# Attention and gated feed-forward on one core: an accumulator on the normalise, sums by column, probability remainders on GpSimd, weight words merged in PSUM, and twelve leading weight blocks

## The chip, the cores and the metric

The kernel runs on one NeuronCore of a Trainium2 chip. The metric is the device time of one execution in microseconds; the median of several runs counts. The engines are named as in the profile: PE is TensorE (PEld its weight loads), DVE is VectorE, ACT is ScalarE, POOL is GpSimd, and SP is SyncE, which issues the DMAs.

## The reference

Eight batches with eight heads of width 64. Each batch has 512 local tokens, which attend to the 32 global tokens and to local tokens within 32 positions, and 32 global tokens, which attend to everything. The result, 544 tokens by 512 per batch, goes through a gated feed-forward layer of width 1536.

```
sm(s):  e = exp(s - max(s));  e / (sum(e) + 1e-9)
out_g = sm(scale * q_g k_all^T) v_all
out_l = sm([scale * q_l k_g^T, scale * q_l k_l^T where |i - j| <= 32 else -1e9]) [v_g; v_l]
x     = all heads of a token side by side
out   = (sigmoid(x w_gate) * (x w_val)) w_out
```

The three weights are fp64 values of which the kernel receives the bits; all else is fp32.

## The kernel before, in words

**Precision.** A product in full fp32 is slow on TensorE, so most operands are split: a "hi" part, rounded to the type float32r by ScalarE, and a "lo" part, the remainder, by a subtraction on GpSimd (`hh lo`, `xt lo`, `k lo`, `q lo`, `v lo`, `p lo`, `w lo`). Three products (hi hi, lo hi, hi lo) replace one.

**Work.** The tokens form chunks: chunk 0 is the first 256 tokens of batch 0, chunk 1 the other 256 with the batch's global tokens, chunks 2 to 8 are batches 1 to 7 of 512 tokens, and at the end come the 256 global tokens of all batches. For each chunk attention makes `xt` (the hi and lo parts of x, transposed), and the feed-forward stream runs over 12 weight blocks f of 128 columns: gate products into `bank_g`, value products into `bank_v` (L705), then the output products of the block before into `bank_o` (L719). While TensorE streams the feed-forward of one chunk, the attention of the next one is woven in.

**Attention of a head** has local units of two blocks of 128 queries (`local_unit`), and a `global_unit`. In the first heads (chunks 0 and 1, half of chunk 2: 24 units, "native") all is in fp32, and TensorE transposes the probabilities. The other 104 units run: scores on PE (L338); mask, scaling and maximum on DVE, which writes `s_buf` and, through its accumulator, `nm` (L376); exponential on ACT with the row sums in `sm` (L389); then the step `norm` on DVE: add 1e-9 to both sums (L433), reciprocal (L434), multiply each block by its reciprocal (L436 twice, 192 or 224 columns), transpose in 32 by 32 blocks into `tb` (L438). Four DMAs write `tb` to DRAM and two read it back as `pt` (L444, L449). ACT takes the hi part (L452), the step `p lo` subtracts it (L454; on DVE for the first unit of a head, on POOL for the second), and PE multiplies by the values (L462, L463). Then ACT copies, DVE adds (L468) and POOL adds (L470) into x.

**Weights.** `convert(i)` turns 36 blocks of fp64 words into fp32 at the start: a DMA brings 512 KB into a part of the tile `xt`; DVE masks the sign (L230) and merges the low word (L231), ACT rescales the high word (L233), DVE merges it (L235); ACT takes the hi part (L242) and POOL the lo part (L244). The output weight's parts go to DRAM (`wo_dram`) and are loaded again for each use (L668).

**The order.** `Order` is a planner that runs when the program is built: each piece of work yields steps with an engine, an assumed duration in us and the buffers it takes and gives, and the planner always begins the step that can start first, with ties by rank. The assumed durations decide how the instructions of each engine are interleaved; on the chip each engine then runs its list in that order. Lines that matter here:

```
LEAD = 8                     # blocks f of chunk 0, then of chunk 1, before the two alternate
items = [(chs[0], f) for f in range(LEAD)] + [(chs[1], f) for f in range(LEAD)]
for f in range(LEAD, NF):    # NF = 12
    items += [(chs[0], f), (chs[1], f)]
RANK = {"split": 1.0, "conv": 15.0, "products": 5.0}
```

Of the kernel before, what the change touches and what calls it, by code (L numbers as in the profile page):

```python
# [16 lines left out]
P = 128  # L17
# [5 lines left out]
KWIN = (192, 224, 224, 192)  # L23
# [122 lines left out]
def kernel(ctx, tc, qk, v, w_gate, w_val, w_out, out_l, out_g):  # L146
    nc = tc.nc
# [12 lines left out]
    ps = ctx.enter_context(tc.tile_pool(name="ps", bufs=1, space=PSUM))  # L160
# [59 lines left out]
    def convert(i):  # L220
        f, kind = divmod(i, 3)
        yield step("load w", "SP", 0.4, take=[f"words{i % 3}"], lat=4.6)
        src = conv_bufs[i % 3]
        nc.sync.dma_start(src, w_src[i])
        yield step("word", "DVE", 0.35 + 0.62, take=[f"out{i % 2}"])
        pairs = src.rearrange("p (n two) -> p n two", two=2)
        low, high = pairs[:, :, 0], pairs[:, :, 1]
        w = conv_out[i % 2]
        wf, hf = w.bitcast(F32), high.bitcast(F32)
        nc.vector.tensor_scalar(w, high, 0x80000000, None, op0=ALU.bitwise_and)  # L230
        nc.vector.scalar_tensor_tensor(w, low, 29, w, op0=ALU.logical_shift_right, op1=ALU.bitwise_or)  # L231
        yield step("exponent", "ACT", 0.58)
        nc.scalar.mul(hf, hf, 2.0 ** -112)  # L233
        yield step("word", "DVE", 0.62, give=[f"words{i % 3}"])
        nc.vector.scalar_tensor_tensor(w, high, 3, w, op0=ALU.logical_shift_left, op1=ALU.bitwise_or)  # L235
        yield step("w hi", "ACT", 0.52, take=["ob", "ob"] if kind == 2 else ())
        if kind == 2:
            hi, lo = (ffn.tile([P, 1, DM], F32R, name=nm, tag="ob", bufs=3) for nm in ("wo_hi", "wo_lo"))
        else:
            hi, lo = (t[:, :, f * P:(f + 1) * P] for t in (wg, wv)[kind])  # L240
        wf = wf.rearrange("p (t n) -> p t n", t=hi.shape[1])
        nc.scalar.copy(hi, wf)  # L242
        yield step("w lo", "POOL", 1.35, give=[f"out{i % 2}"])
        nc.gpsimd.tensor_tensor(lo, wf, hi.bitcast(F32), op=ALU.subtract)  # L244
# [95 lines left out]
    def x_part(T, x32s, col0):  # L340
# [3 lines left out]
        prow = 64 * (h % 2)  # L344
        return x32s[h // 2][prow:prow + 64, col0:col0 + 2 * P].rearrange("p (i c) -> p i c", c=P)

    def first_x(T):
        key = "x", T["h"] // 2
        T["group"][key] = T["group"].get(key, 0) + 1
        return ["x32"] if T["group"][key] == 1 else []  # L350

    def local_unit(T, blocks, x32s, col0):
# [17 lines left out]
        else:  # L370
            si = free_s.pop(0)
            s_sb = s_bufs[si]
# [17 lines left out]
                                 accum_out=sm[:, i:i + 1])  # L390
        if nat:
            yield step("sum", "DVE", 0.38)
            nc.vector.tensor_scalar_add(r, sm, 1e-9)
            nc.vector.reciprocal(r, r)
            for i, j in enumerate(blocks):
                yield (st := step("norm", ("DVE", "ACT"), 0.3))
                src = s_sb[:, i, 0:KWIN[j]]
                if st["eng"] == "ACT":
                    nc.scalar.mul(src, src, r[:, i:i + 1])
                else:  # L400
                    nc.vector.tensor_scalar(src, src, r[:, i:i + 1], None, op0=ALU.mult)
            where = f"o{h % 2}" if T["first"] else "att"
            yield step("turn", "PE", 0.46 + (0.43 if T["first"] else 0.0), take=[where])
            pt_ps = bank([P, 4, P], "bank_y", where)
            if T["first"]:
                warm(pt_ps.rearrange("p a c -> p (a c)"), 4)
            for i in range(2):
                nc.tensor.transpose(pt_ps[:, 2 * i], s_sb[:, i, 0:P], ident)
                nc.tensor.transpose(pt_ps[:, 2 * i + 1], s_sb[:, i, WIN - P:WIN], ident)
            own = "th" if T["first"] and h % 2 else "pt"  # L410
            yield step("pt", "ACT", 0.5, take=[own], give=[where, s_res])
            if own == "th":
                pt = ffn.tile([P, 4, P], F32, name="pt_first", tag="th", bufs=2)
            else:
                pt = att.tile([P, 4, P], F32, name="pt_nat", tag="pt", bufs=2)
            nc.scalar.copy(pt, pt_ps)
            if not own_s:
                free_s.append(si)
            where = f"o{2 + h % 2}" if T["first"] else "att"
            yield step("pv", "PE", 1.1, take=[where] + first_x(T), give=[own] + v_over(T), after=[when(("v", ci, h))])  # L420
            vt = T["group"]["v", h]
            o_ps = bank([64, 2, P], "bank_x", where)
            for i, j in enumerate(blocks):
                side = KWIN[j] - (WIN - P)
                nc.tensor.matmul(o_ps[:, i], vt[:, VM[j], :], pt[:, 2 * i], start=True, stop=False)
                nc.tensor.matmul(o_ps[:, i], vt[0:side, VS[j], :], pt[0:side, 2 * i + 1], start=False, stop=True)
            yield step("x", "ACT", 0.3, give=[where])
            nc.scalar.copy(x_part(T, x32s, col0), o_ps)
            mark(("x", ci, h // 2))
            return  # L430

        yield step("norm", "DVE", 0.38 + 0.5 + 0.6, take=["tb"], give=["s"])
        nc.vector.tensor_scalar_add(r, sm, 1e-9)  # L433
        nc.vector.reciprocal(r, r)  # L434
        for i, j in enumerate(blocks):
            nc.vector.tensor_scalar(s_sb[:, i, 0:KWIN[j]], s_sb[:, i, 0:KWIN[j]], r[:, i:i + 1], None, op0=ALU.mult)  # L436
        tb = att.tile([P, 7, 2, 32], F32, name="tb", bufs=2)
        nc.vector.transpose(tb.rearrange("p b k i -> p k b i"), s_sb.rearrange("p k (b i) -> p k b i", i=32))  # L438
        free_s.append(si)
# [7 lines left out]
        for m in range(2):  # L447
# [2 lines left out]
        yield step("p hi", "ACT", 0.52)  # L450
        flat = pt.rearrange("p c m a k i -> p c (m a k i)")
        nc.scalar.copy(flat[:, 0], flat[:, 1].bitcast(F32))  # L452
        yield (st := step("p lo", "POOL" if blocks[0] else "DVE", 0.85 if blocks[0] else 0.8))
        (nc.vector if st["eng"] == "DVE" else nc.gpsimd).tensor_tensor(  # L454
            flat[:, 1], flat[:, 1].bitcast(F32), flat[:, 0].bitcast(F32), op=ALU.subtract)
# [369 lines left out]
```

## Time and profile before

| | before |
|---|---|
| median of 3 runs | 1236.57 us (1235.94 to 1245.51) |
| profiled execution | 1240.92 us, span 1239.2 us |
| PE busy | 1161.9 us, 94% |
| DVE busy | 824.0 us, 66% |
| ACT busy | 785.0 us, 63% |
| POOL busy | 659.9 us, 53% |
| mean granted clock of PE | 0.989 |

The span goes from the first to the last instruction. A busy PE is not PE at its peak, since the ends of matmuls are modelled, so what it waits for is read beside it. In lists of groups a row names line, engine, operation, tiles and count, then busy us, mean ns of one, and the idle time before it with what ended it. The page slices the span; the table of stretches gives the same engine columns for chosen times.

### The profile page before, as it was taken

What the parts mean: (1) busy time and instruction counts of PE and PEld (TensorE: products, weight loads), DVE (VectorE), ACT (ScalarE), POOL (GpSimd) and SP (SyncE); (2) the same over time, 40 slices, a digit from 0 to 9 for tenths busy, and PEclk for the clock granted to TensorE, in tenths of its full rate; (3) what the DMA queues carried; (4) which work ended last, traced back from release to release, by engine and by line L of the source; (5) the groups of instructions that cost most, each with busy time, mean ns of one, the idle gap of its engine ahead of it and who ended that gap; (6) DMA issues with size and microseconds to landing.
All of it is one profiled execution on the core that took longest, in us unless ns stands there. A gap on an engine that the chain in (4) does not pass through costs nothing.

```text
span 1239.2 us, 20480 instructions
## 1 busy us (share of the span) xinstructions
PE 1161.9 (94%) x6236; PEld 946.4 (76%) x6236; DVE 824.0 (66%) x2318; ACT 785.0 (63%) x1844; POOL 659.9 (53%) x683
## 2 busy tenths in 40 slices
PE   9999889898999999999999998999899999999998
PEld 7777668887777777777777776777677777888897
DVE  3578875866875788768776787678776787521121
ACT  4677876766666676767665776667666776522232
POOL 1244444666666576667656666657656676511111
PEclk9998999999999999999999999999999999999999
DMA  6578765656555666566555664566555664321243
GB/s 212 165 242 262 249 204 152 185 164 172 153 168 157 187 179 159 160 179 181 152 149 156 201 183 143 166 173 179 156 153 143 199 192 125 103 87 66 68 137 119
DMA packets 180077, 204.00 MB, mean 165 GB/s; under 512 B 109312, under 2 KB 136960, under 8 KB 179968
## 3 DMA queue, kind: packets, MB, share of 16 engines
q1 hardware_dynamic: 179968, 202.70, 56.0%
q8 instruction: 49, 0.80, 0.3%
q14 instruction: 60, 0.49, 0.1%
HBM read 163.58 MB, written 39.06 MB: 164 GB/s over the span
## 4 chain that ended last, share of the span: by engine, by line
PE 23%; DVE 13%; DMA 12%; issue 9%; ACT 9%; POOL 5%; SPq 4%; DVEq 0%; POOLq 0%; ACTq 0%
PE bank_o L719 8%; PE bank_v L705 6%; PE bank_g L705 6%; DMA pt<-pd 5%; DMA qk_raw<-in_qk_dram 3%; DMA pd<-tb 3%; DVE s_buf L436 2%; ACT qk_hi L280 2%; ACT s_buf L389 2%; SPq L444 2%; DVE r L433 2%; DVE tb L438 2%; SPq L277 1%; POOL kl L283 1%; POOL pt L454 1%
## 5 line engine op out<-in xcount | busy, mean ns | idle before, releaser
L705 PE MATMUL bank_v<-xt,wv 128*128 128x512 f32 (+1 forms) x1440 | 325.9, 366 | 8.6 <-DVE t L468 7.4
L705 PE MATMUL bank_g<-xt,wg 128*128 128x512 f32 (+1 forms) x1440 | 320.6, 365 | 1.7 <-ACT xt L586 1.1
L719 PE MATMUL bank_o<-wo,hh 128*128 128x512 f32 x1224 | 317.2, 398 | 0.3 <-ACT hh L660 0.2
L705 PEld LDWEIGHTS bank_v<-xt,wv 128*128 128x128 f32 x1440 | 241.0, 190 | 55.9 <-DVE t L468 10.5
L705 PEld LDWEIGHTS bank_g<-xt,wg 128*128 128x128 f32 x1440 | 241.8, 190 | 45.9 <-DVE th L657 3.4
L719 PEld LDWEIGHTS bank_o<-wo,hh 128*128 128x128 f32 x1224 | 223.8, 191 | 44.9 <-issue 1.0
L662 POOL TENSOR_TENSOR hh<-th,hh 128x512 fp32r<-128x512 f32 (+1 forms) x120 | 139.3, 1161 | 211.0 <-ACT hh L660 200.4
L656 DVE SCALAR_TENSOR_TENSOR bank_v<-ex,bank_v 128x512 f32<-128x512 f32 (+1 forms) x120 | 72.2, 602 | 140.5 <-PE bank_v L705 135.9
L389 ACT ACTIVATE s_buf<-s_buf,nm 128x192 f32<-128x192 f32 (+1 forms) x248 | 113.9, 461 | 73.3 <-DVE nm L376 72.7
L283 POOL TENSOR_TENSOR kl<-qk_raw,qk_hi 128x736 fp32r<-128x736 f32 x52 | 95.8, 1842 | 111.6 <-ACT qk_hi L280 101.9
L660 ACT CAST hh<-th 128x512 fp32r<-128x512 f32 (+1 forms) x120 | 66.5, 554 | 106.9 <-DVE th L657 105.3
L470 POOL TENSOR_TENSOR x<-t 64x256 f32<-64x256 f32 x104 | 76.0, 730 | 70.1 <-DVE t L468 34.6
L436 DVE TENSOR_SCALAR s_buf<-s_buf,r 128x192 f32<-128x192 f32 x208 | 106.0, 550 | 3.6
L645 ACT ACTIVATE th<-bank_g 128x512 f32<-128x512 f32 (+1 forms) x120 | 63.8, 532 | 68.1 <-PE bank_g L705 66.1
L376 DVE CUSTOM_DVE_ANT_0 s_buf<-bank_x,masks 128x192 f32<-128x192 f32 (+1 forms) x248 | 81.3, 363 | 26.9 <-PE bank_x L338 25.6
L462 PE MATMUL bank_x<-pt,vhl 128*128 128x256 f32 x208 | 61.1, 314 | 36.4 <-POOL pt L454 22.1
L468 DVE TENSOR_TENSOR t<-bank_x,t 64x512 f32<-64x512 f32 x104 | 69.6, 669 | 36.6 <-ACT t L466 36.5
L466 ACT COPY t<-bank_x 64x512 f32<-64x512 f32 x104 | 60.6, 583 | 47.2 <-POOL x L470 25.9
L433 DVE TENSOR_SCALAR r<-sm 128x2 f32<-128x2 f32 x104 | 54.5, 524 | 48.5 <-ACT s_buf L389 46.1
L452 ACT CAST pt<-pt 128x512 fp32r<-128x512 f32 x104 | 64.1, 616 | 35.4 <-DMA pt<-pd 34.6
L462 PEld LDWEIGHTS bank_x<-pt,vhl 128*128 128x128 f32 x208 | 39.3, 189 | 59.8 <-POOL pt L454 35.5
L286 POOL TENSOR_TENSOR qk_hi<-qk_raw,qk_hi 64x256 fp32r<-64x256 f32 x104 | 82.0, 808 | 4.1
(122 smaller groups left out, 2057.8 us busy)
## 6 DMA issues: line engine op xcount, KB each, us to landing
wo<-wo_dram SPq DMA_DIRECT2D x116, 512.0 KB, 3.6
qk_raw<-in_qk_dram SPq DMA_DIRECT2D x104, 320.0 KB, 4.7
pt<-pd SPq DMA_DIRECT2D x208, 128.0 KB, 2.6
pd<-tb SPq DMA_DIRECT2D x416, 56.0 KB, 1.8
v_raw<-in_v_dram SPq DMA_DIRECT2D x52, 256.0 KB, 3.3
out_dram<-ob SPq DMA_DIRECT2D x34, 256.0 KB, 4.2
xt<-in_w_gate_dram SPq DMA_DIRECT2D x12, 512.0 KB, 4.1
xt<-in_w_val_dram SPq DMA_DIRECT2D x12, 512.0 KB, 4.6
```

What stands on the lines that cost most here:

```text
L283: nc.gpsimd.tensor_tensor(kl, t[:, K0:Q1], hi[:, K0:Q1].bitcast(F32), op=ALU.subtract)
L286: nc.gpsimd.tensor_tensor(hi[64:128, r], t[64:128, r], hi[64:128, r].bitcast(F32), op=ALU.subtract)
L376: nc.vector.tensor_tensor_reduce(out=s_sb[:, i, 0:w], in0=s_ps[:, i, 0:w], in1=masks[:, m:m + w], scale=-0.125, scalar=3.0e38, op0=ALU.add ...
L389: nc.scalar.activation(s_sb[:, i, 0:w], s_sb[:, i, 0:w], AF.Exp, bias=nm[:, i:i + 1], scale=-1.0, accum_out=sm[:, i:i + 1])
L433: nc.vector.tensor_scalar_add(r, sm, 1e-9)
L436: nc.vector.tensor_scalar(s_sb[:, i, 0:KWIN[j]], s_sb[:, i, 0:KWIN[j]], r[:, i:i + 1], None, op0=ALU.mult)
L462: nc.tensor.matmul(out, vt[:, VM[j], :], pt[:, :, 0, :, i, :], start=True, stop=False)
L470: nc.gpsimd.tensor_tensor(x_part(T, x32s, col0), t0[:, :, 0], t0[:, :, 1], op=ALU.add)
L656: nc.vector.scalar_tensor_tensor(acc, ex, 1.0, acc, op0=ALU.min, op1=ALU.mult)
L662: nc.gpsimd.tensor_tensor(hh[:, 1, 0:ntok], th, hh[:, 0, 0:ntok].bitcast(F32), op=ALU.subtract)
L705: nc.tensor.matmul(acc, w[a][:, t, fs], xt[:, c, t, x0:x0 + ntok], start=n == 0, stop=n == 11)
L719: nc.tensor.matmul(C2["o"][t], ph[:, a, t * P:(t + 1) * P], pwo[:, c], start=f2 == 0 and i == 0, stop=f2 == NF - 1 and i == 2)
```

## The change

1. The sums get 1e-9 by column: two adds of 128x1 instead of one of 128x2 (`invert`), then the reciprocal as before.
2. The normalise on DVE, also that of native units, writes an accumulator too (`normalise`); its sum goes to `sm`, which nobody reads afterwards.
3. `p lo` is on POOL for all 104 units, with an assumed 1.28 us (before 0.85 on POOL, 0.8 on DVE); the step `norm` is assumed to take 1.7 us instead of 1.48.
4. In `convert` the words of blocks f < LEAD are merged in a PSUM bank (`bank_w`, the bank o2 or o3); only the last merge writes the tile in SBUF.
5. LEAD is 12, so chunk 0 runs all its blocks before chunk 1 begins, all 36 blocks of words are merged in PSUM, and no block's output weights serve two chunks from one load. The rank of conversions is 5 instead of 15.

```diff
-LEAD = 8
+LEAD = 12
-RANK = {"split": 1.0, "conv": 15.0, "products": 5.0}
+RANK = {"split": 1.0, "conv": 5.0, "products": 5.0}
...
-        yield step("word", "DVE", 0.35 + 0.62, take=[f"out{i % 2}"])
+        early = f < LEAD
+        part = f"o{2 + i % 2}" if early else f"out{i % 2}"
+        yield step("word", "DVE", 0.45 + 0.69, take=[part])
         w = conv_out[i % 2]
-        nc.vector.tensor_scalar(w, high, 0x80000000, None, op0=ALU.bitwise_and)
-        nc.vector.scalar_tensor_tensor(w, low, 29, w, op0=ALU.logical_shift_right, op1=ALU.bitwise_or)
+        v = ps.tile([P, 512], F32, name="bank_w", tag=f"bank_{part}").bitcast(U32) if early else w
+        nc.vector.tensor_scalar(v, high, 0x80000000, None, op0=ALU.bitwise_and)
+        nc.vector.scalar_tensor_tensor(v, low, 29, v, op0=ALU.logical_shift_right, op1=ALU.bitwise_or)
         yield step("exponent", "ACT", 0.58)
...
-        nc.vector.scalar_tensor_tensor(w, high, 3, w, op0=ALU.logical_shift_left, op1=ALU.bitwise_or)
+        nc.vector.scalar_tensor_tensor(w, high, 3, v, op0=ALU.logical_shift_left, op1=ALU.bitwise_or)
...
+    def invert(r, sums):
+        for i in range(2):
+            nc.vector.tensor_scalar_add(r[:, i:i + 1], sums[:, i:i + 1], 1e-9)
+        nc.vector.reciprocal(r, r)
+
+    def normalise(p, r, total):
+
+        nc.vector.tensor_scalar(p, p, r, None, op0=ALU.mult, op1=ALU.add, accum_out=total)
...
-        yield step("norm", "DVE", 0.38 + 0.5 + 0.6, take=["tb"], give=["s"])
-        nc.vector.tensor_scalar_add(r, sm, 1e-9)
-        nc.vector.reciprocal(r, r)
+        yield step("norm", "DVE", 0.4 + 0.7 + 0.6, take=["tb"], give=["s"])
+        invert(r, sm)
         for i, j in enumerate(blocks):
-            nc.vector.tensor_scalar(s_sb[:, i, 0:KWIN[j]], s_sb[:, i, 0:KWIN[j]], r[:, i:i + 1], None, op0=ALU.mult)
+            normalise(s_sb[:, i, 0:KWIN[j]], r[:, i:i + 1], sm[:, i:i + 1])
...
-        yield (st := step("p lo", "POOL" if blocks[0] else "DVE", 0.85 if blocks[0] else 0.8))
-        (nc.vector if st["eng"] == "DVE" else nc.gpsimd).tensor_tensor(
-            flat[:, 1], flat[:, 1].bitcast(F32), flat[:, 0].bitcast(F32), op=ALU.subtract)
+        yield step("p lo", "POOL", 1.28)
+        nc.gpsimd.tensor_tensor(flat[:, 1], flat[:, 1].bitcast(F32), flat[:, 0].bitcast(F32), op=ALU.subtract)
```

How the instructions stand now is shown at three places; in each fence the line numbers are those of its own kernel. First DVE, the `norm` step of a unit in the middle of the program, before:

```order
L433 TENSOR_SCALAR r<-sm 128x2
L434 RECIPROCAL r<-r 128x2
L436 TENSOR_SCALAR s_buf_106<-s_buf_106,r 128x224
L436 TENSOR_SCALAR s_buf_106<-s_buf_106,r 128x192
L438 STREAM_TRANSPOSE tb<-s_buf_106 128x2x7x32
```

And with the change, at the same unit:

```order
L353 TENSOR_SCALAR r<-sm 128x1 x2
L354 RECIPROCAL r<-r 128x2
L358 TENSOR_SCALAR s_buf_106,sm<-s_buf_106,r 128x224
L358 TENSOR_SCALAR s_buf_106,sm<-s_buf_106,r 128x192
L449 STREAM_TRANSPOSE tb<-s_buf_106 128x2x7x32
```

The sums are two instructions, and each normalise has a second output.

Second POOL, in the middle of the program, from one `p lo` (pt) to the next, before:

```order
L454 TENSOR_TENSOR pt<-pt 128x512
L662 TENSOR_TENSOR hh<-th,hh 128x512
L470 TENSOR_TENSOR x_4489<-t_4533 64x256
L502 TENSOR_TENSOR xg_113<-y 64x32
L283 TENSOR_TENSOR kl<-qk_raw,qk_hi 128x736
L571 TENSOR_TENSOR ptg<-ptg_buf,ptg 128x5x32
L470 TENSOR_TENSOR x_4489<-t_4617 64x256
L286 TENSOR_TENSOR qk_hi<-qk_raw,qk_hi 64x256
L286 TENSOR_TENSOR qk_hi<-qk_raw,qk_hi 64x288
L454 TENSOR_TENSOR pt<-pt 128x512
```

And with the change:

```order
L465 TENSOR_TENSOR pt<-pt 128x512
L581 TENSOR_TENSOR ptg<-ptg_buf,ptg 128x5x32
L290 TENSOR_TENSOR qk_hi<-qk_raw,qk_hi 64x256
L290 TENSOR_TENSOR qk_hi<-qk_raw,qk_hi 64x288
L465 TENSOR_TENSOR pt<-pt 128x512
L480 TENSOR_TENSOR x_5488<-t_5642 64x256
L672 TENSOR_TENSOR hh<-th,hh 128x512
L318 TENSOR_TENSOR vhl<-v_raw,vhl 128x8x64
L480 TENSOR_TENSOR x_5488<-t_5705 64x256
L512 TENSOR_TENSOR xg_113<-y 64x32
L465 TENSOR_TENSOR pt<-pt 128x512
```

POOL's list now has a `p lo` for each unit, two in a head, between the same other subtractions and adds.

Third PE, the probability products of one unit (pt by vhl) among the feed-forward of the third 512-token chunk, before:

```order
L719 MATMUL bank_o_6581<-wo,hh 128x512
L705 MATMUL bank_g<-xt,wg_114 128x512 x4
L462 MATMUL bank_x<-pt,vhl 128x256
L463 MATMUL bank_x<-pt,vhl 128x256
L462 MATMUL bank_x<-pt,vhl 128x256
L463 MATMUL bank_x<-pt,vhl 128x256
L705 MATMUL bank_g<-xt,wg_115 128x512 x4
L479 MATMUL bank_x<-ptg,vhl 128x64
```

And with the change, at the same rows of the list:

```order
L729 MATMUL bank_o_6684<-wo,hh 128x512
L715 MATMUL bank_g<-xt,wg_114 128x512 x4
L715 MATMUL bank_g<-xt,wg_115 128x512 x4
L472 MATMUL bank_x<-pt,vhl 128x256
L473 MATMUL bank_x<-pt,vhl 128x256
L472 MATMUL bank_x<-pt,vhl 128x256
L473 MATMUL bank_x<-pt,vhl 128x256
L489 MATMUL bank_x<-ptg,vhl 128x64
```

The four products stand behind one more group of four gate matmuls; the unit before this one moved by one group of four value matmuls in the same way. Scores stand where they stood.

More of the change, by code (lines that the diff above doesn't have):

```diff
@@ L224, in convert @@
         nc.sync.dma_start(src, w_src[i])
-        yield step("word", "DVE", 0.35 + 0.62, take=[f"out{i % 2}"])
         pairs = src.rearrange("p (n two) -> p n two", two=2)
         low, high = pairs[:, :, 0], pairs[:, :, 1]
+        hf = high.bitcast(F32)
+        early = f < LEAD
+        part = f"o{2 + i % 2}" if early else f"out{i % 2}"
+        yield step("word", "DVE", 0.45 + 0.69, take=[part])
         w = conv_out[i % 2]
-        wf, hf = w.bitcast(F32), high.bitcast(F32)
-        nc.vector.tensor_scalar(w, high, 0x80000000, None, op0=ALU.bitwise_and)
-        nc.vector.scalar_tensor_tensor(w, low, 29, w, op0=ALU.logical_shift_right, op1=ALU.bitwise_or)
+        v = ps.tile([P, 512], F32, name="bank_w", tag=f"bank_{part}").bitcast(U32) if early else w
+        nc.vector.tensor_scalar(v, high, 0x80000000, None, op0=ALU.bitwise_and)
+        nc.vector.scalar_tensor_tensor(v, low, 29, v, op0=ALU.logical_shift_right, op1=ALU.bitwise_or)
         yield step("exponent", "ACT", 0.58)
         nc.scalar.mul(hf, hf, 2.0 ** -112)
-        yield step("word", "DVE", 0.62, give=[f"words{i % 3}"])
-        nc.vector.scalar_tensor_tensor(w, high, 3, w, op0=ALU.logical_shift_left, op1=ALU.bitwise_or)
+        yield step("word", "DVE", 0.69, take=[f"out{i % 2}"] if early else [], give=[f"words{i % 3}"] + ([part] if early else []))
+        nc.vector.scalar_tensor_tensor(w, high, 3, v, op0=ALU.logical_shift_left, op1=ALU.bitwise_or)
+        wf = w.bitcast(F32)
         yield step("w hi", "ACT", 0.52, take=["ob", "ob"] if kind == 2 else ())
@@ L400, in local_unit @@
                 else:
-                    nc.vector.tensor_scalar(src, src, r[:, i:i + 1], None, op0=ALU.mult)
+                    normalise(src, r[:, i:i + 1], sm[:, i:i + 1])
             where = f"o{h % 2}" if T["first"] else "att"
@@ L430, in local_unit @@
             return
-        yield step("norm", "DVE", 0.38 + 0.5 + 0.6, take=["tb"], give=["s"])
-        nc.vector.tensor_scalar_add(r, sm, 1e-9)
-        nc.vector.reciprocal(r, r)
+        yield step("norm", "DVE", 0.4 + 0.7 + 0.6, take=["tb"], give=["s"])
+        invert(r, sm)
         for i, j in enumerate(blocks):
-            nc.vector.tensor_scalar(s_sb[:, i, 0:KWIN[j]], s_sb[:, i, 0:KWIN[j]], r[:, i:i + 1], None, op0=ALU.mult)
+            normalise(s_sb[:, i, 0:KWIN[j]], r[:, i:i + 1], sm[:, i:i + 1])
         tb = att.tile([P, 7, 2, 32], F32, name="tb", bufs=2)
```

## The prediction

> **What bounds the kernel now.** I read the engine totals first, then three stretches of the span (the weight conversion, the long middle, the tail without attention), and then what TensorE waited for in the middle.
>
> ```profile
> span 1239.2 us, 20480 instructions
> PE 1161.9 (94%) x6236; PEld 946.4 (76%) x6236; DVE 824.0 (66%) x2318; ACT 785.0 (63%) x1844; POOL 659.9 (53%) x683
> ```
>
> ```profile
> 0.00:200.00 200.00, 184.97 (x1097) 146.85 (x1098) 133.48 (x370) 142.32 (x383) 75.63 (x83) 0.96 0.68 214
> 200.00:1062.00 862.00, 804.42 (x4251) 653.81 (x4251) 651.81 (x1877) 586.13 (x1339) 547.42 (x562) 0.99 0.60 167
> 1062.00:1240.00 178.00, 172.51 (x890) 145.70 (x889) 38.70 (x73) 56.56 (x124) 36.87 (x39) 1.00 0.28 95
> ```
>
> The columns are PE, PEld, DVE, ACT and POOL busy, granted clock, DMA share and GB/s. TensorE sets the time, and the change leaves its matmuls alone, so a gain can come only from its idle time and lowered clock. In the middle that is 862.0 - 804.4 = 57.6 us of idle time plus 0.01 x 862, about 9 us, of clock; in the first 200 us it is 15.0 us plus 0.04 x 200 = 8 us. The tail has 5.5 us, and nothing there is touched.
>
> ```profile
> PE bank_x L462 <- POOL pt L454: 22.1, 32, 2.9
> PE bank_x L462 <- issue: 10.8, 13, 1.3
> PE bank_v L705 <- DVE t L468: 7.4, 7, 1.5
> PE bank_x L462 <- DVE pt L454: 3.1, 4, 1.5
> ```
>
> These are the largest waits of TensorE between 200 and 1062 us (us, times, longest). L462 is the first matmul of probabilities by values. Its three rows make 36.0 us, most of the 57.6. It ends a long chain: scores, reduce, exponential, normalise and transpose (VectorE), two trips through DRAM, high part (ScalarE), remainder (L454). TensorE's order is fixed beforehand, so whenever this chain is later than its step times foresaw, all matmuls behind L462 stand still.
>
> Why is it late? The next rows give durations as minimum/median/maximum ns.
>
> ```profile
> L433 DVE TENSOR_SCALAR r<-sm x104: 160/507/1726, 201.6 to 1058.5; 128x2 f32<-128x2 f32 x104
> L436 DVE TENSOR_SCALAR s_buf<-s_buf,r x208: 305/337/1373, 202.0 to 1059.6; 128x192 f32<-128x192 f32 x52, 128x224 f32<-128x224 f32 x52
> L454 DVE TENSOR_TENSOR pt<-pt x52: 684/693/2219, 212.0 to 1066.8; 128x512 fp32r<-128x512 f32 x52
> L438 DVE STREAM_TRANSPOSE tb<-s_buf x104: 645/645/648, 203.2 to 1060.0; 128x448 f32<-128x448 f32 x104
> L547 DVE TENSOR_SCALAR mg<-sg x64: 131/142/145, 60.4 to 1064.1; 32x1 f32<-32x1 f32 x64
> L468 DVE TENSOR_TENSOR t<-bank_x,t x104: 643/674/684, 217.4 to 1072.9; 64x512 f32<-64x512 f32 x104
> L454 POOL TENSOR_TENSOR pt<-pt x52: 1255/1288/1312, 217.6 to 1068.4; 128x512 fp32r<-128x512 f32 x52
> ```
>
> The first three spread by a factor of three to ten on equal work; the next three do not spread at all. What the first three have in common is that all their large operands lie in SBUF. One place shows what they wait for:
>
> ```profile
> 750.71 0.48 DVE L433 TENSOR_SCALAR r<-sm 128x2 f32<-128x2 f32 x1
> 751.43 2.51 DVE L436 TENSOR_SCALAR s_buf<-s_buf,r 128x192 f32<-128x192 f32 x2
> 753.98 0.65 DVE L438 STREAM_TRANSPOSE tb<-s_buf 128x448 f32<-128x448 f32 x1
> 751.25 1.29 POOL L454 TENSOR_TENSOR pt<-pt 128x512 fp32r<-128x512 f32 x1
> 752.50 1.31 POOL L662 TENSOR_TENSOR hh<-th,hh 128x512 fp32r<-128x512 f32 x1
> ```
>
> Two normalises, at least 0.31 + 0.32 us, take 2.51 us and end just after the two GpSimd subtractions beside them (751.25 to 753.81). VectorE is held for whole GpSimd instructions. The means give the price:
>
> ```profile
> L433 DVE TENSOR_SCALAR r<-sm 128x2 f32<-128x2 f32 x104 | 54.5, 524 | 48.5 <-ACT s_buf L389 46.1
> L436 DVE TENSOR_SCALAR s_buf<-s_buf,r 128x192 f32<-128x192 f32 x104 | 56.4, 542 | 1.8
> L436 DVE TENSOR_SCALAR s_buf<-s_buf,r 128x224 f32<-128x224 f32 x104 | 58.0, 557 | 1.8
> L434 DVE RECIPROCAL r<-r 128x2 f32<-128x2 f32 x104 | 17.2, 166 | 3.6
> L454 DVE TENSOR_TENSOR pt<-pt 128x512 fp32r<-128x512 f32 x52 | 45.1, 867 | 10.7 <-ACT pt L452 10.3
> ```
>
> A unit's step from L433 to L438 is 0.52 + 0.17 + 0.54 + 0.56 + 0.65 = 2.44 us; without holding it is 0.16 + 0.17 + 0.31 + 0.33 + 0.65 = 1.62. So 0.82 us per unit, 85 us over 104 units, is holding, and the step time that set the order was 1.48.
>
> **The change part by part.** *Normalise and sums.* Two column adds replace one pair add: by L547 about 0.14 each, so 0.30 with the second's start. The accumulating normalise is not in the trace. To bound it I compare two SBUF instructions of the conversion:
>
> ```profile
> L230 DVE TENSOR_SCALAR xt<-xt x36: 407/424/1868, 12.7 to 171.8; 128x512 uint32<-128x512 uint32 x36
> L231 DVE SCALAR_TENSOR_TENSOR xt<-xt x36: 691/693/1672, 13.1 to 173.7; 128x512 uint32<-128x512 uint32 x36
> ```
>
> L231 handles the same 512 columns 0.27 us slower, 0.53 ns a column. If the accumulating form also falls to that rate, the normalises become 0.31 + 0.10 = 0.41 and 0.33 + 0.12 = 0.45, plus the read of the accumulator:
>
> ```profile
> L376 DVE DVE_READ_ACCUMULATOR2_ANT nm<- 128x1 f32 x256 | 20.9, 82 | 0.0
> ```
>
> At 0.08 each, of which one is hidden, the unit is 0.30 + 0.17 + 0.41 + 0.45 + 0.08 + 0.65 = 2.06 us if nothing holds it, against 2.44: **0.38 us less**, 40 us in all. The ends are 0.82 less (full rate, no holding) and 0.44 more (slow rate and all the holding as now). I take 0.38, because the accumulating reductions on L376 show no holding in their rows (0.33 to 0.39 us), though they read PSUM.
>
> [...]
>
> *Remainders.* 52 subtractions leave VectorE (0.867 us each, 45 us) for GpSimd at 1.288, so these units' chains get 0.42 us longer, and GpSimd's middle goes from 547 to about 614 of 862 us, 71%. The step times now say 1.28 where the GpSimd half was planned at 0.85. In the order, at the place shown with the change, both probability matmuls stand one group of four feed-forward matmuls later, 4 x 0.233 = 0.93 us (the tail runs twelve in 2.80 us):
>
> ```profile
> 1083.30 2.80 PE bank_v L705 x12
> ```
>
> *What TensorE gets back in the middle.* A head has two units. Its chains give back 2 x 0.38 and lose 0.42, which leaves 0.34 us; where the matmuls also stand up to 0.93 us later, up to 1.9 us per head is covered. Today the L462 waits are 36.0 / 52 = 0.69 us per head. I take three quarters of them, 27 us. Of the other 21.6 us of idle time I take 8, since VectorE's middle loses about 80 of 652 us and it frees the score and value banks (L705 behind L468). Of the 9 us of clock I take 4, on the guess that its dips follow long waits. Together **-39 us**; the bounds are nothing and the whole 66.
>
> *The conversion.* Its three word instructions and the sums on native heads are held too:
>
> ```profile
> L230 DVE TENSOR_SCALAR xt<-xt 128x512 uint32<-128x512 uint32 x36 | 22.7, 631 | 24.7 <-DMA xt<-in_w_gate_dram 12.7 <-POOL wg L244 10.2 <-POOL wo_lo L244 1.5
> L231 DVE SCALAR_TENSOR_TENSOR xt<-xt 128x512 uint32<-128x512 uint32 x36 | 29.6, 823 | 1.2
> L235 DVE SCALAR_TENSOR_TENSOR xt<-xt 128x512 uint32<-128x512 uint32 x36 | 29.5, 826 | 10.8 <-ACT xt L233 10.8
> 80.00:180.00 100.00, 90.11 (x588) 68.12 (x587) 87.14 (x215) 82.62 (x223) 45.39 (x40) 0.95 0.78 243
> ```
>
> Means of 0.631, 0.823 and 0.826 against about 0.42, 0.69 and 0.68 make 0.49 us per word block, 18 us over 36. Writing PSUM is not shown for them; if the first falls to L231's rate it costs 0.27 x 36 = 10 us. So VectorE, 87% busy here, gains 8 to 18 us. With LEAD at 12 chunk 0 needs all 36 blocks before chunk 1 starts, and four more loads of 512 KB are issued:
>
> ```profile
> wo<-wo_dram SPq DMA_DIRECT2D x116, 512.0 KB, 3.6
> ```
>
> At the 243 GB/s of this stretch they are 4 x 2.2 = 9 us of transfers, hidden by the 22% of free DMA time unless they queue ahead of weight loads. I take **-8 us** of the 23 on offer, bounds +8 to -18.
>
> Sum: -47 us. The profiled execution took 1240.92 us, its span and 1.7 around it, so 1194; it lies 4.35 above the median of the runs, so the forecast is **1190 us**.
>
> **The rivals.** *GpSimd becomes the bound (slower).* Place: the remainder of the units that ran on VectorE. It is 71% busy then and works in order, and there the subtraction stands behind hh, kl and qk_hi work (the order shows it; the pt and hh rows above give 1.3 us). If each of the 52 waits one such instruction more, say 1.3 us, its chain gets 1.7 us longer while the head's two normalises give back 0.76 and the later place 0.93. From there on more waiting goes straight to TensorE: at 2.2 us of extra waiting it is 0.9 x 52 = 47 us lost against perhaps 20 gained elsewhere, so 1264 us. For it: L462 waits for POOL seven times as long as for DVE. Against it: GpSimd in the middle still waits over a third of the time, and its step time is now right. Chance 7%.
>
> *The accumulating form is held as well.* Then only the sums (0.22 x 104 = 23 us of VectorE), the removed subtraction and the better step time count, while slower normalises take 23 us back: about -8 us, 1229 us. Chance 8%. *DMA keeps the chain late.* The chain's DRAM trips stay:
>
> ```profile
> pt<-pd SPq DMA_DIRECT2D x208, 128.0 KB, 2.6
> pd<-tb SPq DMA_DIRECT2D x416, 56.0 KB, 1.8
> ```
>
> If those are what L462 really ends on, half the middle's gain goes, 1210 us: 20%. *Waits nearly vanish*, since planned and real times now agree everywhere: -85 us, about 1152: 7%.
>
> **How the numbers follow.** My forecast has 58%, DMA 20%, vanishing waits 7%, held accumulation 8%, GpSimd 7%. The range is 1155 to 1225: it takes in the forecast with its bounds and the DMA case and leaves the two unfavourable cases and the far end of the favourable one outside, some 2 in 10. A measurement here tells 1%, 12 us, from no change (1224 to 1249). Faster 0.85 (the first three cases), same 0.08, slower 0.07.
>
> **What would show it.** In the profile after: the accumulating normalise at 0.4 to 0.46 us with hardly any spread, column adds at 0.14; VectorE busy near 720 us (824 less 40, 45 and about 18) and GpSimd near 715 (660 plus 67, less its own share of the holding); L462 waiting under 15 us in all; the granted clock nearer 1 in the first 200 us. I am wrong if normalises still reach 1.3 us, if the waits on L454 grow while GpSimd never idles, or if L705 waits for weight blocks of f = 8 to 11 before chunk 1.

## The result, and the profile after

The changed kernel takes **1195.36 us** (median of 4 runs, 1192.61 to 1199.26) against 1236.40 before: a ratio of 0.9653, 95% interval 0.9599 to 0.9708. The forecast was 1190, its range 1155 to 1225. Run again later, beside the experiments, the same kernel took 1196.83 us (1187.77 to 1202.50), ratio 0.9667 [0.9609, 0.9724]. Medians are over all runs; a ratio and its interval are estimated from the runs that do not count as slow, and are not the quotient of the medians. The profiled execution took 1192.61 us.

The engine totals of the page after:

```profile
span 1190.8 us, 20839 instructions
PE 1142.7 (96%) x6236; PEld 943.1 (79%) x6236; DVE 722.7 (61%) x2625; ACT 778.6 (65%) x1842; POOL 708.2 (59%) x735
```

VectorE fell from 824.0 to 722.7 us and GpSimd rose from 659.9 to 708.2 (forecast 720 and 715). The same three stages after, in the columns of the table before (PE, PEld, DVE, ACT and POOL busy, clock, DMA share, GB/s):

```profile
0.00:190.00 190.00, 181.00 (x1125) 144.56 (x1126) 125.92 (x431) 143.88 (x389) 74.08 (x85) 0.98 0.69 228
190.00:1013.00 823.00, 788.44 (x4222) 652.23 (x4221) 558.70 (x2125) 577.95 (x1329) 596.00 (x610) 0.99 0.64 177
1013.00:1191.00 178.00, 173.23 (x893) 146.31 (x892) 38.04 (x73) 56.73 (x125) 38.10 (x40) 0.99 0.28 95
```

The middle lasts 823 us instead of 862, minus 39, and the stage ahead of it ends some 10 us sooner; the tail is as long as before. TensorE idles 34.6 us in the middle, where it idled 57.6. Only 23 of the 39 us are therefore idle time; the other 16 stood in the column of busy PE (804.4 before, 788.4 now), whose matmul ends are modelled. The two windows do not hold quite the same matmuls (4251 and 4222). Counted from the first feed-forward matmul of chunk 2 (266.4 and 257.0 us) to the same ends, with 3788 and 3785 matmuls, the stretch lost 39.6 us: 25.2 idle and 14.4 busy.

What TensorE waits for after, over the whole span (us, times, longest):

```profile
PE bank_x L472 <- POOL pt L465: 21.7, 20, 3.1
PE bank_g L715 <- DVE th L667: 3.3, 3, 1.1
PE bank_o L729 <- DVE ob L687: 2.5, 3, 1.0
...
PE bank_v L715 <- DVE t L478: 1.9, 4, 0.6
```

L472 is what L462 was. Its three rows made 36.0 us; one is left, with 21.7. The wait for GpSimd alone has hardly changed (22.1 before).

The instructions that the change writes anew (count, minimum/median/maximum ns, first and last start, shapes):

```profile
L353 DVE TENSOR_SCALAR r<-sm x256: 131/154/157, 16.3 to 1009.3; 128x1 f32<-128x1 f32 x128
L358 DVE TENSOR_SCALAR_CACHE_REDUCE s_buf<-s_buf,r x225: 396/425/449, 17.2 to 1010.1; 128x224 f32<-128x224 f32 x57, 128x192 f32<-128x192 f32 x56
L358 DVE DVE_READ_ACCUMULATOR s_buf<-s_buf,r x225: 71/83/90, 17.6 to 1010.4; 128x1 f32 x113
L465 POOL TENSOR_TENSOR pt<-pt x104: 1256/1292/1311, 199.8 to 1020.5; 128x512 fp32r<-128x512 f32 x104
L233 DVE TENSOR_SCALAR bank_w<-xt x36: 662/689/696, 12.4 to 152.2; 128x512 uint32<-128x512 uint32 x36
L234 DVE SCALAR_TENSOR_TENSOR bank_w<-xt,bank_w x36: 695/695/701, 13.2 to 152.9; 128x512 uint32<-128x512 uint32 x36
L238 DVE SCALAR_TENSOR_TENSOR xt<-xt,bank_w x36: 656/680/689, 23.0 to 154.4; 128x512 uint32<-128x512 uint32 x36
```

Each minimum is close to its maximum. Before, the pair add ran up to 1.73 us, the normalise to 1.37 and the word instructions to 1.87. One place shows the normalise beside GpSimd:

```profile
746.08 1.29 POOL L465 TENSOR_TENSOR pt<-pt 128x512 fp32r<-128x512 f32 x1
746.14 0.41 DVE L358 TENSOR_SCALAR_CACHE_REDUCE s_buf<-s_buf,r 128x192 f32<-128x192 f32 x1
...
746.48 0.44 DVE L358 TENSOR_SCALAR_CACHE_REDUCE s_buf<-s_buf,r 128x224 f32<-128x224 f32 x1
...
746.97 0.65 DVE L449 STREAM_TRANSPOSE tb<-s_buf 128x448 f32<-128x448 f32 x1
```

Both normalises run inside one GpSimd subtraction that reads and writes SBUF, and neither side is longer for it. Over the whole trace 115 of the 229 normalises lie inside GpSimd arithmetic with at least 95% of their length and take 0.426 us on average; 42 lie outside it with at least 95% and take 0.422.

### The profile page after: what moved, and what is told of

It is laid out like the page before. It is cut to its first block, busy times and chain, and to the rows that moved or that the text cites. A ratio compares the mean times of both kernels' runs of the same rounds, so it can differ in the third digit from the quotient of the medians.

```text
span 1190.8 us, 20839 instructions
## 1 busy us (share of the span) xinstructions
PE 1142.7 (96%) x6236; PEld 943.1 (79%) x6236; DVE 722.7 (61%) x2625; ACT 778.6 (65%) x1842; POOL 708.2 (59%) x735
## 5 line engine op out<-in xcount | busy, mean ns | idle before, releaser
L715 PE MATMUL bank_v<-xt,wv 128*128 128x512 f32 (+1 forms) x1440 | 321.9, 365 | 3.8 <-DVE t L478 1.9
L729 PE MATMUL bank_o<-wo,hh 128*128 128x512 f32 x1224 | 321.3, 398 | 4.0 <-DVE ob L687 2.5
L715 PEld LDWEIGHTS bank_v<-xt,wv 128*128 128x128 f32 x1440 | 238.6, 190 | 49.2 <-DVE mg L550 5.0
L672 POOL TENSOR_TENSOR hh<-th,hh 128x512 fp32r<-128x512 f32 (+1 forms) x120 | 135.0, 1125 | 186.6 <-ACT hh L670 171.0
L465 POOL TENSOR_TENSOR pt<-pt 128x512 fp32r<-128x512 f32 x104 | 134.2, 1291 | 55.0 <-ACT pt L463 47.8
L287 POOL TENSOR_TENSOR kl<-qk_raw,qk_hi 128x736 fp32r<-128x736 f32 x52 | 92.5, 1778 | 33.7 <-ACT qk_hi L284 29.1
L480 POOL TENSOR_TENSOR x<-t 64x256 f32<-64x256 f32 x104 | 76.1, 732 | 48.2 <-DVE t L478 17.8
L318 POOL TENSOR_TENSOR vhl<-v_raw,vhl 128x512 fp32r<-128x512 f32 x52 | 67.1, 1290 | 44.6 <-ACT vhl L316 36.5
L358 DVE TENSOR_SCALAR_CACHE_REDUCE s_buf<-s_buf,r 128x192 f32<-128x192 f32 (+1 forms) x225 | 88.2, 427 | 3.9
L463 ACT CAST pt<-pt 128x512 fp32r<-128x512 f32 x104 | 64.0, 616 | 39.3 <-DMA pt<-pd 39.2
L667 DVE SCALAR_TENSOR_TENSOR th<-th,bank_v 128x512 f32<-128x512 f32 (+1 forms) x120 | 73.0, 608 | 15.5 <-ACT th L658 5.8
L290 POOL TENSOR_TENSOR qk_hi<-qk_raw,qk_hi 64x256 fp32r<-64x256 f32 x104 | 78.4, 775 | 4.1
```

What stands on the lines that cost most here:

```text
L287: nc.gpsimd.tensor_tensor(kl, t[:, K0:Q1], hi[:, K0:Q1].bitcast(F32), op=ALU.subtract)
L290: nc.gpsimd.tensor_tensor(hi[64:128, r], t[64:128, r], hi[64:128, r].bitcast(F32), op=ALU.subtract)
L358: nc.vector.tensor_scalar(p, p, r, None, op0=ALU.mult, op1=ALU.add, accum_out=total)
L465: nc.gpsimd.tensor_tensor(flat[:, 1], flat[:, 1].bitcast(F32), flat[:, 0].bitcast(F32), op=ALU.subtract)
L480: nc.gpsimd.tensor_tensor(x_part(T, x32s, col0), t0[:, :, 0], t0[:, :, 1], op=ALU.add)
L667: nc.vector.scalar_tensor_tensor(th, th, 1.0, acc, op0=ALU.add, op1=ALU.mult)
```

## The experiments

Each was run in three rounds beside the kernel before, whose median was 1235.31 us with the first four, 1236.49 with the next three and 1235.13 with the last four. Line numbers are those of the changed kernel, except where the kernel before was edited.

### One part undone: the accumulator, the column sums

```diff
-        nc.vector.tensor_scalar(p, p, r, None, op0=ALU.mult, op1=ALU.add, accum_out=total)
+        nc.vector.tensor_scalar(p, p, r, None, op0=ALU.mult)
```

> The changed kernel with its normalise without the accumulator; every engine's order is that of the changed kernel, so only the form of 229 instructions differs. Theory (holding by GpSimd): normalises are held again, mean 0.55 to 0.65 us with maxima over 1.2, against 0.41 and 0.44; VectorE about 20 us busier; 1195 becomes about 1212 us (1205 to 1225). Rival (the new order brought the gain): within 5 us of 1195, since uncontended normalises are shorter without the accumulator (0.32 against 0.43).

Measured: 1214.18 us (1209.25 to 1216.37), ratio 0.9826 [0.9766, 0.9885]. The normalise, in the same order of instructions:

```profile
L358 DVE TENSOR_SCALAR s_buf<-s_buf,r x225: 306/339/2017, 17.4 to 1034.2; 128x224 f32<-128x224 f32 x57, 128x192 f32<-128x192 f32 x56
```

The result is what my theory expected, except that VectorE is 29 us busier (751.3 against 722.7) where 20 were expected. The minimum is 0.09 us shorter than with the accumulator, the maximum 1.6 us longer.

```diff
-        for i in range(2):
-            nc.vector.tensor_scalar_add(r[:, i:i + 1], sums[:, i:i + 1], 1e-9)
+        nc.vector.tensor_scalar_add(r, sums, 1e-9)
```

> The changed kernel with one 128x2 add for both sums instead of two 128x1 adds; same order on every engine. Theory (holding): the add means 0.5 us with maxima over 1.2, against 2 x 0.15; about 0.2 us more on each of 128 units' chains; 1195 becomes 1203 us (1198 to 1212). Rival (the order hides it): within 4 us of 1195.

Measured: 1215.46 us (1212.66 to 1216.71), ratio 0.9839 [0.9782, 0.9895]: 12 us more than expected. The pair add:

```profile
L352 DVE TENSOR_SCALAR r<-sm x128: 149/259/1641, 16.0 to 1033.4; 128x2 f32<-128x2 f32 x128
```

The expectation compared instruction means (as measured, 0.444 us against two of 0.150). What the chain feels is the time from the end of a unit's second exponential, when both sums are there, to the end of its transpose. I worked it out from the traces as a mean over the 104 units: before 2.82 us, changed 2.19, without the accumulator 2.50, with pair sums 2.52. Each of the two edits alone thus loses 0.31 to 0.32 us per unit and 19 to 20 us in all. An add of two columns thus weighs as much as two whole normalises. The expectation also left out that, of two column adds, the first is mostly done before the second sum is there.

### One part undone: remainders, words, LEAD

```diff
-        yield step("p lo", "POOL", 1.28)
-        nc.gpsimd.tensor_tensor(flat[:, 1], ...
+        yield (st := step("p lo", "POOL" if blocks[0] else "DVE", 1.28 if blocks[0] else 0.8))
+        (nc.vector if st["eng"] == "DVE" else nc.gpsimd).tensor_tensor(flat[:, 1], ...
```

> The changed kernel with the probability remainders of each head's first unit back on VectorE (assumed 0.8 us there, 1.28 on GpSimd, so the order is planned anew). Theory (holding): the 52 subtractions are held, mean about 0.9 us with maxima near 2, and GpSimd's subtractions are held too, up to 1.8; 1195 becomes 1203 us (1195 to 1215). Rival (GpSimd's longer subtraction is what now makes TensorE wait): faster, 1188 us (1180 to 1194).

Measured: 1205.18 us (1193.91 to 1208.81), ratio 0.9768 [0.9698, 0.9839]. Its interval overlaps that of the change, so what this part is worth (about 9 us by the medians) is not settled. The one traced execution, the fastest of the four, points the same way: from the first feed-forward matmul of chunk 2 to that of chunk 8 it takes 783.1 us, where two executions of the change take 775.1 and 776.5. The row of the 52 remainders on VectorE:

```profile
L465 DVE TENSOR_TENSOR pt<-pt x52: 647/796/3928, 194.1 to 1019.3; 128x512 fp32r<-128x512 f32 x52
```

A subtraction of 0.65 us that reads two SBUF operands was held for up to 3.28 us; its mean was 1.066.

```diff
-        early = f < LEAD
+        early = False
```

> The changed kernel with all weight words merged in SBUF again, LEAD still 12. Theory (holding in the conversion): the first merges mean 0.6 to 0.8 us with maxima over 1.5, and what is lost is lost before 190 us: 1195 becomes 1202 us (1196 to 1210). Rival (the conversion is covered there, and writing PSUM costs 0.26 us on each first instruction): within 4 us of 1195 or faster.

Measured: 1203.56 us (1192.46 to 1209.02), ratio 0.9734 [0.9658, 0.9810]; again the interval overlaps that of the change, so the 8 us between the medians are what was expected but not shown. The holding is plain: L234 averaged 0.914 us against 0.696 and L238 0.814 against 0.677, while L233 was cheaper in SBUF, 0.637 against 0.686. The traces, one execution each, show where the time went. With the words in SBUF the feed-forward of chunk 2 starts at 267.2 us, in two executions of the change at 257.0 and 258.6; from there to the feed-forward of chunk 8 the three take 773.4, 775.1 and 776.5 us. So that execution lost its time in the conversion, as expected.

```diff
-LEAD = 12
+LEAD = 8
```

> The changed kernel with LEAD 8: the words of blocks 8 to 11 are merged in SBUF, chunks 0 and 1 alternate over those blocks, four loads of output weights fewer. Theory (holding counts, the lead does not): within 6 us of the changed kernel, 4 us slower at the most likely, since 12 of 36 blocks are held again. Rival (the lead brought gain of its own in the first 190 us): 10 us slower or more.

Measured: 1195.10 us (1194.44 to 1195.61), ratio 0.9659 [0.9624, 0.9695]. LEAD makes no difference that can be measured here. The edit also merges the words of 12 blocks in SBUF again, so two small effects that cancel are not excluded.

### The instructions without the order, the order without the instructions

The kernel before, with the new sums and the accumulating normalise and nothing else, so that all other instructions keep their places:

```diff
-        nc.vector.tensor_scalar_add(r, sm, 1e-9)
+        for i in range(2):
+            nc.vector.tensor_scalar_add(r[:, i:i + 1], sm[:, i:i + 1], 1e-9)
...
-            nc.vector.tensor_scalar(s_sb[...], s_sb[...], r[:, i:i + 1], None, op0=ALU.mult)
+            nc.vector.tensor_scalar(s_sb[...], s_sb[...], r[:, i:i + 1], None, op0=ALU.mult,
+                                    op1=ALU.add, accum_out=sm[:, i:i + 1])
```

> The kernel before with the two column adds and the accumulating normalise in the 104 split units, nothing else; the assumed step times and so the order are those of before. Theory (holding on the chain): the middle gains most of its 39 us in the old order too; 1236 becomes 1207 us (1198 to 1216). Rival (the new assumed times and the remainder's place in the order brought half or more): 1220 us or more.

Measured: median 1203.72 us (1186.79 to 1206.32), ratio 0.9662 [0.9565, 0.9759]. These few instructions give most of the gain in the old order. The traces agree: from the feed-forward of chunk 2 to that of chunk 8 the kernel before takes 813.9 us, this one 777.5 and the change 775.1. TensorE's waits for probabilities (L464 there) were then:

```profile
PE bank_x L464 <- POOL pt L456: 19.1, 28, 1.8
...
PE bank_x L464 <- issue: 4.8, 9, 0.9
...
PE bank_x L464 <- DVE pt L456: 2.0, 3, 1.0
```

With one row more, of 0.4 us, that is 26.3 us instead of 36.0. The converse leaves all instructions of before as they were and gives the planner the step times that the trace of before shows:

```diff
-        yield step("norm", "DVE", 0.38 + 0.5 + 0.6, take=["tb"], give=["s"])
+        yield step("norm", "DVE", 2.44, take=["tb"], give=["s"])
...
-        yield (st := step("p lo", "POOL" if blocks[0] else "DVE", 0.85 if blocks[0] else 0.8))
+        yield (st := step("p lo", "POOL" if blocks[0] else "DVE", 1.29 if blocks[0] else 0.87))
```

> The kernel before with assumed times as measured and no other edit: the step norm 2.44 us instead of 1.48, p lo 1.29 on GpSimd and 0.87 on VectorE instead of 0.85 and 0.80. All holding stays. Theory (holding is lost time that an order cannot give back, since it varies from 1.6 to 4.1 us): TensorE's waits before probability products shrink, but 1236 becomes no better than 1225 us (1215 to 1236). Rival (it is the order): 1212 us or less.

Measured: 1196.12 us (1190.36 to 1197.49), ratio 0.9659 [0.9616, 0.9702], as fast as the change, with all the holding left in it:

```profile
L436 DVE TENSOR_SCALAR s_buf<-s_buf,r x208: 306/336/3062, 189.8 to 1010.8; 128x192 f32<-128x192 f32 x52, 128x224 f32<-128x224 f32 x52
```

```profile
PE bank_x L462 <- POOL pt L454: 6.3, 9, 2.2
...
PE bank_x L462 <- issue: 2.4, 5, 1.3
...
PE bank_x L462 <- DVE pt L454: 1.1, 1, 1.1
```

With one row more, of 0.3 us, the waits for probabilities are down from 36.0 us to 10.1. My theory that an order cannot give the holding back fell here. The reading that fits both kernels is that TensorE loses the gap between how long the chain takes and how much of TensorE's own work the order puts between a unit's scores and its products; a truer step time closes that gap as well as a shorter chain does. The experiments below show that this is not all. The new order also starts the feed-forward of chunk 2 at 255.1 us, with the words still merged in SBUF, so PSUM is not the only way to that gain.

### Both: the change with a longer assumed step time

```diff
-        yield step("norm", "DVE", 0.4 + 0.7 + 0.6, take=["tb"], give=["s"])
+        yield step("norm", "DVE", 2.06, take=["tb"], give=["s"])
```

> The changed kernel with the step norm assumed at 2.06 us instead of 1.70. Theory (TensorE waits where a chain is later than assumed): the waits before probability products, 21.7 us in the changed kernel, fall under 12 us and 1196 becomes 1188 us (1180 to 1195). Rival (what is left is variation of the DRAM trips, which no mean corrects): within 5 us of 1196 and those waits above 18 us.

Measured: **1178.31 us** (1175.93 to 1180.65), ratio 0.9530 [0.9471, 0.9589]: the fastest kernel here, its interval below that of the change. Its page and its stages:

```profile
span 1174.9 us, 20835 instructions
PE 1136.9 (97%) x6236; PEld 943.5 (80%) x6236; DVE 720.0 (61%) x2622; ACT 783.8 (67%) x1845; POOL 708.0 (60%) x735
```

```profile
190.00:1006.00 816.00, 792.22 (x4269) 660.56 (x4269) 561.37 (x2137) 589.19 (x1345) 600.09 (x616) 1.00 0.65 180
```

```profile
PE bank_x L472 <- POOL pt L465: 10.0, 13, 2.3
PE bank_v L715 <- ACT ex L656: 7.1, 6, 1.4
PE bank_v L715 <- DVE t L478: 3.4, 5, 1.1
```

One number in the planner, 1.70 to 2.06, halves the wait on L472 (21.7 to 10.0 us). TensorE's idle time in the middle is 23.8 us. The 2.06 us were the estimate of the prediction. The step as measured in the changed kernel, from the last add to the end of the transpose, takes 1.86 us, so 1.70 was 0.16 too short and 2.06 is 0.20 too long; counted from the second exponential, with the waits for VectorE, the mean is 2.19. This run thus shows that a longer assumed time helps, not that the true one is best: 1.86 was not run. If all time went with the clock, the mean granted clocks of the two kernels' runs (0.990 and 0.993) would account for about 3 of the 17 us, an estimate. The same instructions matter under better orders too: the kernel before with true step times is 18 us slower (1196.12 us).

### Holding that is foreseen, and more of the truth

The plain, held normalise again (as in the first experiment), now with a longer time for the step in the planner:

```diff
-        nc.vector.tensor_scalar(p, p, r, None, op0=ALU.mult, op1=ALU.add, accum_out=total)
+        nc.vector.tensor_scalar(p, p, r, None, op0=ALU.mult)
...
-        yield step("norm", "DVE", 0.4 + 0.7 + 0.6, take=["tb"], give=["s"])
+        yield step("norm", "DVE", 2.26, take=["tb"], give=["s"])
```

> The changed kernel without the accumulator (1214 us so far) and with the step norm assumed at its measured 2.26 us instead of 1.70. Theory (not the holding but the gap between assumed and real time costs): 1214 becomes 1198 us (1190 to 1205) although normalises are held as before. Rival (held time is lost whatever is assumed): 1209 us or more.

Measured: 1208.99 us (1205.12 to 1210.84), ratio 0.9774 [0.9714, 0.9835]. By the medians the longer time gave back 5 us of what the holding had cost, and the intervals of the two kernels overlap, so even that is not settled. The result lies outside the theory's range and at the rival's bound of 1209 us: here the holding itself costs. The holding was foreseen only in part, since in this order the step took 2.43 us (1.61 to 4.33), not 2.26. What TensorE waits for has changed:

```profile
PE bank_v L715 <- DVE mg L550: 20.8, 11, 3.0
PE bank_x L472 <- POOL pt L465: 19.2, 23, 2.9
PE bank_x L472 <- issue: 5.9, 6, 1.6
```

In the changed kernel the first row is 1.8 us. L550 is the reduction of the global rows' scores, and the timeline shows how it comes late:

```profile
730.49 1.28 POOL L672 TENSOR_TENSOR hh<-th,hh 128x512 fp32r<-128x512 f32 x1
...
730.57 3.26 DVE L358 TENSOR_SCALAR s_buf<-s_buf,r 128x224 f32<-128x224 f32 x2
...
731.73 0.77 POOL L480 TENSOR_TENSOR x<-t 64x256 f32<-64x256 f32 x1
732.46 1.26 POOL L318 TENSOR_TENSOR vhl<-v_raw,vhl 128x512 fp32r<-128x512 f32 x1
733.87 0.65 DVE L449 STREAM_TRANSPOSE tb<-s_buf 128x448 f32<-128x448 f32 x1
734.43 0.70 DVE L550 CUSTOM_DVE_ANT_0 pg_buf<-bank_x,masks,mg 32x512 f32<-32x512 f32 x1
...
735.20 4.47 PE L715 MATMUL bank_v<-xt,wv 128*128 128x512 f32 x12 [2.98 <-DVE mg L550]
```

Two normalises of 0.31 and 0.32 us last 3.26 us, until the third of three GpSimd instructions ends (730.49 to 733.72). The transpose and the reduction stand behind them, and twelve matmuls of the feed-forward wait 2.98 us for the reduction. Holding here comes in pieces of whole GpSimd instructions: in the trace of before, 83 of the 208 normalises take over 0.49 us, and each of the 83 ends 0.11 to 0.14 us after a GpSimd instruction does. That a mean in the planner cannot foresee which of VectorE's later steps a piece will hit is my explanation of the cost; no run isolates it.

Last, the assumed time of the read back from DRAM was raised too, once in the fastest kernel and once in the kernel before with true step times:

```diff
-        yield step("read", "SP", 0.95, take=["pt"], give=["pd"], lat=3.4)
+        yield step("read", "SP", 0.95, take=["pt"], give=["pd"], lat=4.8)
```

> The changed kernel with norm at 2.06 us and the DRAM read's landing at 4.8 us instead of 3.4, since the measured way from transpose to high part is about 9.1 us and the assumed one 7.7. Theory: the waits before probability products fall under 6 us; 1196 becomes 1184 us (1174 to 1192). Rival (later products only move the wait to the values' banks and to x at the end of a chunk): 1192 us or more.

> The kernel before with norm 2.44, p lo 1.29 and 0.87, and the DRAM read's landing 4.8 us; instructions as before, all holding stays. Theory (gap alone): no worse than 1196 us and within 8 us of the same order correction on the changed kernel. Rival (with a true order the holding itself shows, since VectorE is 100 us busier): 10 us or more behind it.

Measured: 1190.48 us (1186.08 to 1196.91), ratio 0.9633 [0.9563, 0.9703], and 1218.69 us (1215.49 to 1222.58), ratio 0.9867 [0.9795, 0.9940]. Both are slower than without this edit, by 12 and 23 us between the medians; their runs and those without the edit do not overlap. In the first the theory failed although 1190 lies in its range: the waits before probability products were to fall under 6 us and are 22.6. In the second the theory failed too, and its rival holds: it is 28 us behind the first, where 10 or more were named. In the first, what ScalarE waited for ahead of the cast of the high part (L463), without and then with the longer assumed read:

```profile
  DMA pt<-pd: 30.9, 33
```

```profile
  DMA pt<-pd: 17.7, 19
```

With the longer read assumed, ScalarE has to wait for the data in only 19 cases instead of 33, since the cast now stands behind more of ScalarE's other work. The span from the end of the transpose to the start of the cast grew from 9.0 us to 10.6, so the real chain stretched along with the assumption. In the second, the waits for probabilities are 12.9 us, little more than without the edit (10.1), but two others rose:

```profile
PE bank_v L705 <- DVE mg L540: 11.5, 11, 1.3
PE bank_o L719 <- DVE ob L677: 10.0, 5, 2.6
```

Why these two rose by so much is open. Part of both losses may be the clock. The mean granted clock over the runs was 0.9885 with the edit and 0.9928 without in the first, 0.9835 and 0.9918 in the second; if all time went with it, that would be about 5 of the 12 us and 10 of the 23, an estimate.

### All of them side by side

For each profiled execution I worked out the chain (first score matmul of a unit to the end of its remainder; the two units of a head apart) and TensorE's own work in that stretch: the matmuls that its order puts between a unit's scores and its first product, each at the undisturbed pitch of its shape (0.233 us for 128x512). "L472 waits" is the sum of the rows for the probability products, "idle" the span less busy PE.

| kernel | chain, us | own work, us | short by | L472 waits | idle | time, us |
|---|---|---|---|---|---|---|
| before | 18.6 / 19.2 | 16.7 / 16.7 | 1.8 / 2.6 | 36.0 | 77.3 | 1236 |
| new norm and sums, old order | 17.6 / 18.4 | 16.7 / 16.7 | 0.9 / 1.7 | 26.3 | 52.3 | 1204 |
| old instructions, true times | 18.1 / 19.8 | 17.2 / 18.6 | 0.9 / 1.2 | 10.1 | 51.7 | 1196 |
| the change | 18.0 / 18.6 | 16.8 / 17.4 | 1.2 / 1.1 | 21.7 | 48.1 | 1195 |
| without accumulator | 18.5 / 19.1 | 16.8 / 17.4 | 1.7 / 1.7 | 24.6 | 63.1 | 1214 |
| held but foreseen | 19.0 / 19.3 | 17.8 / 18.3 | 1.2 / 1.0 | 25.1 | 65.5 | 1209 |
| change, norm 2.06 | 18.0 / 18.5 | 17.5 / 17.6 | 0.5 / 0.8 | 10.3 | 38.0 | 1178 |
| the same, read 4.8 | 19.9 / 20.6 | 19.0 / 19.7 | 0.9 / 0.9 | 22.6 | 46.3 | 1190 |
| old instructions, true times, read 4.8 | 20.4 / 19.4 | 19.1 / 18.1 | 1.3 / 1.3 | 12.9 | 65.6 | 1219 |

The shortfall orders the fastest and the slowest correctly, but not the rows between. "Held but foreseen" falls no shorter than the change and takes 14 us longer, and the last row falls little shorter than the third and takes 23 us longer. In both slower kernels normalises are held, and waits stand at other banks: `bank_v` waits 20.8 and 11.5 us for the reduction of the global rows, 1.8 in the change and 5.3 in the third row. So the gap explains the waits for probabilities in part, and holding costs beside it.

## Why the prediction was right, and where it was not

*Middle, -39 us: it came out at -39, from other terms, and that the two agree is luck.* The waits on L462 were to give 27 of 36 us and gave 14; the forecast of under 15 us for L472 failed, it is 21.7. The other idle time was to give 8 and gave 9. The clock was to give 4 and gave nothing: it is 0.99 in the middle, as before. What was not in the sum is the 16 us by which busy PE fell. I had argued that a gain could come only from idle time and clock; the busy column held waits too: the same matmuls at nearly the same clock were busy for some 14 us less. The stages add up to 48 us between the two profiled executions, close to the forecast of 47; the medians differ by 41, since the traced execution before was 4.5 us above its median and the one after 2.8 below.

*The unit's step, 2.06 us against 2.44: mis-sized, in my disfavour.* Counted from when both sums are there, as the single add before was, the step from the last add to the end of the transpose takes 1.86 us after (1.83 to 1.86) against 2.46. I had put both column adds on the path, 0.30 us; one of them runs ahead, before the second sum. So 0.60 us per unit is saved, not 0.38.

*Where the rest of that went.* The chain, as a mean over both units of a head, fell only from 18.91 to 18.30 us. Its pieces, worked out from the same units: the wait of the reduction for VectorE fell by 1.00 us, which the sum had left out, and the step by 0.63 (with the wait ahead of it). Given back were 0.42 between reduction and exponential, 0.44 from the transpose to the cast (8.6 and 8.8 us before, 9.1 and 9.2 after, for the two units), and 0.21 in the remainder, which takes 1.29 instead of 0.87 us on 52 units, as forecast; its wait for GpSimd changed by -0.06. Of the DRAM rival this much was right: the trips stay and grew a little. Against this shorter chain the order now sets 0.1 and 0.8 us more of TensorE's own work, where I had counted up to 0.93 for both. So 1.2 us per unit stay uncovered, of 2.2 before. The planner's 1.70 us for this step is 0.16 below the measured 1.86; with 2.06, above it, the wait on L472 halved.

*The accumulating form is not held: right.* It was argued from reductions that read PSUM. The prediction's common mark of the held instructions, large operands in SBUF, does not separate them: the transpose L438 works on SBUF alone and stayed at 645 to 648 ns. The accumulating normalise takes 0.396 to 0.449 us with hardly any spread, on average 0.426 inside GpSimd's work and 0.422 outside it, against up to 2.02 us in the plain form. Why the accumulator makes this difference, no run here shows.

*Conversion, -8 us.* The feed-forward of chunk 2 starts at 257.0 us instead of 266.4, which is -9.4. The clock does not explain it: up to there it was 0.968 before, and 0.973 and 0.947 in the two executions of the change. The mask of the sign, the first word instruction, takes 0.686 us into PSUM, the dearer of the two cases. That the words bring this gain is supported by the trace without them (267.2), though the run times of the two kernels overlap; of LEAD and its four loads no effect was measured. The rank of the conversions, 5 instead of 15, was not undone by itself.

*GpSimd as the bound: did not come.* It is busy 596.0 of 823 us in the middle, 72%, where 71% was forecast. A remainder of the units that were on VectorE starts on average 0.40 us after its cast, before 0.65; for the other unit of a head it is 1.29 instead of 1.16, against the 2.2 us of extra waiting from which the rival would have decided. *Held accumulation* fell with the rows above. *Waits nearly vanish* did not come: the wait on L472 is 21.7 us, and the best order tried here reached 1178 us, not 1152.

## What to carry to other kernels

Where one engine holds another up, look at the spread of equal instructions, not their mean: a form that is about a third slower at its best (0.396 against 0.306 us) and was never held here can win, and a two-column add (held up to 1.64 us) deserves the same look as a large one. After making a step shorter, compare the planner's time for it with the measured one, counted from when its last input is there, try times around it, and go by the result: raising one number was worth 17 us here, and setting one more to its measured value took 12 away. An assumed wait is no neutral fact: work that follows it is put behind other work, and the chain then really takes longer (here 10.6 us from transpose to cast instead of 9.0).

## What the hardware showed that was not expected

A 128x1 add on SBUF was not held at all (0.131 to 0.157 us over 256), while the 128x2 add of the same data took 0.149 us at its shortest and was held up to 1.64; no run here shows why the two differ. The same kernel's granted clock between 100 and 200 us was 0.97 in one profiled execution and 0.93 in another, about 4 us of a span of 1191. Single runs of this kernel lie up to 15 us apart (1187.77 to 1202.50); the mean clocks of these two runs, 0.994 and 0.989, would be about 6 us of that, an estimate, and the rest is open. The spread is more than the differences of 8 to 9 us that stay open above.
